# Linear attention and two dense layers on one core: scores in four array parts, one state run moved, states in other banks, weight loads later

## The chip, the cores and the metric

The kernel runs on one NeuronCore of a Trainium2 chip. Its engines work side by side, each through its own instructions in order: TensorE (PE in the profile; PEld is its weight load), VectorE (DVE), ScalarE (ACT), GpSimd (POOL), and SyncE (SP), which issues nearly all DMA transfers here. SBUF is the core's memory; PSUM has eight banks of 128 x 512 float32 that TensorE writes to. The metric is the device time of one execution in microseconds, lower is better.

## The reference

```python
for b in range(12):                       # blocks of 64 positions; 2 batches, 8 heads, 64 dims
    intra = einsum('bhic,bhjc->bhij', qb, kb) * Dmask      # Dmask = lam ** (i - j), i >= j
    intra = einsum('bhij,bhjd->bhid', intra, vb)
    inter = einsum('bhid,bhde->bhie', qb * lam_pow, kv_state)
    out[b] = intra + inter
    kv_state = lam_block * kv_state + einsum('bhsd,bhse->bhde', kb * rev_pow, vb)
x = out as 1536 x 512
g = elu(x @ w_in)                         # w_in 512 x 2048
x = g @ w_out                             # w_out 2048 x 512
x = softplus(x @ w_in2) @ w_out2          # the same shapes
```

## The kernel before

The attention is done in 12 chunks of 128 positions, six for each batch, with 8 heads as 4 pairs. For a chunk, `att_s` (line 296) makes the scores: 8 float32 matmuls of 64 rows and 128 columns, the even head of a pair from partitions 0 to 63 and the odd one from 64 to 127, into two PSUM banks of `ps_y`. `att_mask` multiplies them on VectorE with the decay mask (line 319). `att_x` (line 323) makes the output transposed in two banks of the ring `ps_h` of four: first the part from the state ("inter", line 334), in 64x64 parts of the array, which the first chunk of a batch does not have, then the part inside the chunk ("intra", line 343). `att_conv` splits the output into a high part on ScalarE (`xh`, line 357) and a rest on VectorE (`xl`, line 358). `att_state` (line 360) makes keys times values (line 370), VectorE adds the faded old state (line 376), GpSimd fades the new one; the last chunk of a batch makes no state. GpSimd scales the next q (`att_prep`), ScalarE (line 284) and GpSimd (line 291) scale the next k.

The order is written out by hand: `attention()` (line 539) issues for chunk g the scores and masking of chunk g+1, its scalings, then x, state and conversion of chunk g. The program order is the order on each engine. A float32 matmul shows as two records in the trace.

Behind the attention stand the two dense layers. Each of their matmuls is done in three products of a high part and a rest (lines 407 to 409 and 480). The weights come as packed words; for each, ScalarE converts twice (lines 111, 112), VectorE shifts and rounds up (lines 116, 122), ScalarE makes the high part (line 125) and VectorE the rest (line 128). Before the first steps of the MLP this is done in halves of a weight (`split_half`, five pieces), and `PIECES` says how many of the pieces of which half stand ahead of `att_x` and behind the conversion in each chunk. (0, 0) is the first half of weight 0, which `m1(0)` needs, (1, 0) that of weight 1. The halves of steps 0 to 4 of the MLP are split inside `early_step`. The first Relu (line 418) and what follows it on ScalarE stand behind the high part of (2, 0).

`LOADS` orders all loads on SyncE's queue: ("q", g) is q and k of a chunk transposed, ("k", g) is k and v, ("w", f, i) half i of weight f; each is 512 KB. The numbers ahead of the lists are the chunks behind which they are issued.

Of the kernel before, what the change touches and what calls it, by code (L numbers as in the profile page):

```python
# [7 lines left out]
F32 = mybir.dt.float32  # L8
# [7 lines left out]
P = 128  # L16
B, H, S, D = 2, 8, 768, 64
NPAIR = H // 2
CPB = S // P
NCHUNK = B * CPB  # L20
# [3 lines left out]
TT = 512  # L24
# [12 lines left out]

LOADS = {
# [4 lines left out]
}  # L43

STARTS = (
# [3 lines left out]
def body(ctx, tc, consts, attqk, attkv, w1, w2, out):  # L49
    nc = tc.nc  # L50
    V, A, G, T = nc.vector, nc.scalar, nc.gpsimd, nc.tensor
# [9 lines left out]
    ps_y = ctx.enter_context(tc.tile_pool(name="ps_y", bufs=1, space=PSUM))  # L61
# [16 lines left out]
    def bank(name):  # L78
        return ps_h.tile([P, TT], F32, tag="h", name=name)
# [89 lines left out]
    def split_half(fc, i):  # L169
        r, c = [x[:, :DM] for x in conv_tiles()]  # L170
        convert(whalf.pop((fc, i)), r, c)
        yield
        shift(r)
        yield
        round_up(r, c)
        yield
        if (fc, 0) not in wh:
            weight_tiles(fc)
        high(r, wh[fc, i])
        yield  # L180
        rest(c, wh[fc, i], wl[fc, i])
# [3 lines left out]
    def half(fc, i, count):  # L185
        if (fc, i) not in halves:
            halves[fc, i] = split_half(fc, i)
        for _ in range(count):
            next(halves[fc, i], None)
# [13 lines left out]
    def setup():  # L203
        A.dma_start(out=const_t, in_=consts)
        A.preload_act_table_set("natural_log_exp_and_others")
        warm(8)
        loads(0)

    def decays():
        for h in range(H):  # L210
            V.tensor_tensor_scan(  # L211
                out=dmask[:, h % 2, h // 2, :], data0=lam_t[:, h:h + 1].to_broadcast([P, P]), data1=id_t,
                initial=0.0, op0=ALU.mult, op1=ALU.add,
            )
        for e in range(2):
            A.activation(out=kdecay[:, e::2], in_=dmask[:, e, :, P - 1], func=AF.Copy)

    def powers():
        G.tensor_copy(qpow[:, :, :1], lam_t[:, H:].unsqueeze(2))
        for w in (1, 2, 4, 8, 16, 32, 64):  # L220
            G.tensor_tensor(
                out=qpow[:, :, w:2 * w], in0=qpow[:, :, :w],
                in1=qpow[:, :, w - 1:w].to_broadcast([P, NPAIR, w]), op=ALU.mult,
            )
# [6 lines left out]
    def loads(g):  # L231
        for load in LOADS.get(g, ()):
            {"q": att_load, "k": att_load_kv, "w": load_half}[load[0]](*load[1:])
# [27 lines left out]
    def att_prep(g):  # L261

        if g < NCHUNK and g % CPB:
            q = at[g][0].rearrange("p (a i) -> p a i", a=NPAIR)
            G.tensor_tensor(out=q, in0=q, in1=qpow, op=ALU.mult)


    def att_turn_k():
        ps = bank("kps")
        for p in range(NPAIR):  # L270
            o = slice(P * p, P * p + P)
            T.matmul(ps[:, o], at[0][1][:, o], id_t, start=True, stop=True, is_transpose=True, skip_group_check=True)  # L272
        return ps

    def k_heads(g):
        return H if g < 3 else H // 2

    def att_prep_k(g, source=None):
        if g >= NCHUNK or g % CPB == CPB - 1:
            return  # L280
        k = at[g][2].rearrange("p (h d) -> p h d", h=H)
        y = k if source is None else source.rearrange("p (h d) -> p h d", h=H)
        for h in range(k_heads(g)):
            A.activation(out=k[:, h], in_=y[:, h], func=AF.Copy, scale=kdecay[:, h:h + 1])

    def att_prep_k2(g):
        if g >= NCHUNK or g % CPB == CPB - 1 or k_heads(g) == H:
            return
        k = at[g][2].rearrange("p (h d) -> p h d", h=H)
        r = slice(k_heads(g), H)  # L290
        G.tensor_tensor(
            out=k[:, r], in0=k[:, r], in1=kdecay[:, r].unsqueeze(2).to_broadcast([P, H - k_heads(g), D]), op=ALU.mult)
# [3 lines left out]
    def att_s(g):  # L296

        if g >= NCHUNK:
            return
        q, k = at[g][:2]  # L300
        ps = [ps_y.tile([P, 512], F32, tag=f"y{g % 2 * 2 + e}", name=f"sps{e}") for e in range(2)]
        for p in range(NPAIR):
            o = slice(P * p, P * p + P)
            for e in range(2):
                r = slice(64 * e, 64 * e + 64)
                T.matmul(ps[e][:, o], k[r, o], q[r, o], start=True, stop=True, skip_group_check=True)  # L306
        sc[g] = ps

    def att_mask(g):
        if g >= NCHUNK:  # L310
            return
        ps = sc[g]
        sc[g] = s = ap2.tile([P, 2, NPAIR, P], F32, tag="sc", name="sc")
        part = 2 if g == 0 else NPAIR
        for a in range(0, NPAIR, part):
            r = slice(a, a + part)
            for e in range(2):
                y = ps[e].rearrange("p (a i) -> p a i", a=NPAIR)
                V.tensor_tensor(out=s[:, e, r], in0=y[:, r], in1=dmask[:, e, r], op=ALU.mult)
# [3 lines left out]
    def att_x(g):  # L323
        a = at[g]
        ps = [bank("xps") for e in range(2)]
        first = g % CPB == 0

        for p in range(0 if first else NPAIR):
            i = slice(P * p, P * p + P)
            o = slice(P * (p // 2), P * (p // 2) + P)  # L330
            for e in range(2):
                r = slice(64 * e, 64 * e + 64)
                c = 64 * (e ^ p & 1)
                T.matmul(  # L334
                    ps[e][c:c + 64, o], state[g - 1][r, p, :], a[0][r, i],
                    start=(p < 2), stop=False, skip_group_check=True,
                )
        for p in range(NPAIR):
            o = slice(P * (p // 2), P * (p // 2) + P)
            for c in range(2):  # L340
                e = c ^ p & 1
                h = 2 * p + e
                T.matmul(  # L343
                    ps[e][64 * c:64 * c + 64, o], a[3][:, D * h:D * h + D], sc[g][:, e, p, :],
                    start=first, stop=True, skip_group_check=True,
                )
        return ps
# [12 lines left out]
    def att_state(g):  # L360

        if g % CPB == CPB - 1:
            return
        a = at[g]
        ps = bank("stps")[:, :NPAIR * D]
        for p in range(NPAIR):
            for e in range(2):
                r = slice(D * e, D * e + D)
                o = slice(P * p + D * e, P * p + D * e + D)
                T.matmul(ps[r, D * p:D * p + D], a[2][:, o], a[3][:, o], start=True, stop=True, skip_group_check=True)  # L370
        ps = ps.rearrange("p (a i) -> p a i", a=NPAIR)
        state[g] = ap2.tile([P, NPAIR, D], F32, tag="state", name="state")
        if g % CPB == 0:
            V.tensor_copy(state[g], ps)
        else:
            V.tensor_tensor(out=state[g], in0=ps, in1=faded.pop(g - 1), op=ALU.add)  # L376
        if g % CPB < CPB - 2:
            faded[g] = ap2.tile([P, NPAIR, D], F32, tag="faded", name="faded")
            decay = qpow[:, :, P - 1:P].to_broadcast([P, NPAIR, D])
            G.tensor_tensor(out=faded[g], in0=state[g], in1=decay, op=ALU.mult)  # L380
# [153 lines left out]

    PIECES = {5: ((), (0, 0)), 6: ((0, 0), ()), 7: ((0, 0), ()), 8: ((0, 0), (1, 0)), 9: ((1, 0), ()), 10: ((1, 0), ()), 11: ((1, 0), ())}

    def attention():
        setup()  # L540
        powers()
        decays()
        att_s(0)
        att_prep_k(0, att_turn_k())
        att_mask(0)
        for g in range(NCHUNK):
            before, behind = PIECES.get(g, ((), ()))
            att_s(g + 1)
            att_mask(g + 1)
            att_prep(g + 1)  # L550
            att_prep_k2(g + 1)
            if before:
                half(*before, 1 if g in (6, 9) else 2)
            ps = att_x(g)
            att_state(g)
            att_conv(g, ps)
            att_prep_k(g + 1)
            if behind:
                half(*behind, 1)
            loads(g or None)  # L560
# [101 lines left out]
```

## Time and profile before

| | us |
|---|---|
| three runs | 571.41, 571.55, 571.59 (median 571.55) |
| the profiled execution | 571.56 |
| its span in the trace | 569.4 |
| TensorE busy | 563.9 (99%) |
| ScalarE / VectorE / GpSimd busy | 361.2 / 341.8 / 164.8 |
| attention, up to the first MLP matmul | 42.82 |

The time of an execution has 2.16 us around the span. [...] The DMA queue is full from 10 to 44 us (page part 2 and the windows: a share of 1.03 and 406 to 411 GB/s from 10 to 40 us). In the timeline a row is a group of like instructions: start, length to the end of the last, engine, line, operation, written tile <- read tiles, array part, shape, count; in brackets the idle time ahead of it and what ended that.

### The profile page before, as it was taken

To read this page: it belongs to the slowest core of one execution; us is meant where nothing else is said; L and a number is where in the kernel's file an instruction comes from. 1 tells how busy PE (TensorE), PEld (TensorE's weight loads), DVE (VectorE), ACT (ScalarE), POOL (GpSimd) and SP (SyncE) were. 2 spreads that over 40 slices of the span, in tenths; PEclk is the share of its full clock that TensorE was granted. 3 is DMA by queue.
4 is the path that set the end of the run, shared out by engine and by line. 5 is a ranking of instruction groups with operands and counts; after the bars stand their busy time and mean duration, and the time that the engine had idled before them with its cause. 6 is when DMAs were issued, how large, how long until landed. Compare 5 with 4: busy or idle time off the path is not lost.

```text
span 569.4 us, 7780 instructions
## 1 busy us (share of the span) xinstructions
PE 563.9 (99%) x3031; PEld 468.9 (82%) x3031; DVE 341.8 (60%) x407; ACT 361.2 (63%) x597; POOL 164.8 (29%) x143
## 2 busy tenths in 40 slices
PE   9999999999999999999999999999999999999997
PEld 8888888888888888888888888888888888888886
DVE  6797445545464444012767867665789855656656
ACT  5569657756566564333886976756899756655562
POOL 4661312222122122531532442122221221222210
PEclk9999999999999999999999999999999999999999
DMA  8992211423123222000332101100232000100202
GB/s 325 407 406 81 102 74 75 147 87 136 75 76 146 74 74 75 1 1 1 148 122 101 74 12 63 49 26 2 79 143 74 2 0 1 74 1 0 75 0 74
DMA packets 10692, 49.58 MB, mean 87 GB/s; under 512 B 1184, under 2 KB 1568, under 8 KB 7072
## 3 DMA queue, kind: packets, MB, share of 16 engines
q1 hardware_dynamic: 10368, 48.89, 22.7%
q8 instruction: 23, 0.38, 0.3%
q10 hardware_dynamic: 288, 0.20, 0.2%
q14 instruction: 13, 0.11, 0.1%
HBM read 45.95 MB, written 3.15 MB: 86 GB/s over the span
## 4 chain that ended last, share of the span: by engine, by line
PE 98%; DVE 1%; DMA 0%; issue 0%; DVEq 0%
PE y L480 45%; PE hps L407 15%; PE hps L409 15%; PE hps L408 15%; PE sps L306 2%; PE xps L343 2%; PE xps L334 1%; PE stps L370 1%; DMA const_t<-consts 0%; DVE dmask L211 0%; DVE yacc L527 0%; DVE yacc L482 0%; PE kps L272 0%; DVE state L376 0%; DVE yacc L519 0%
## 5 line engine op out<-in xcount | busy, mean ns | idle before, releaser
L407 PE MATMUL hps<-xh,wh 128*128 128x512 f32 x384 | 149.5, 389 | 0.0
L409 PE MATMUL hps<-xh,wl 128*128 128x512 f32 x384 | 149.5, 389 | 0.0
L408 PE MATMUL hps<-xl,wh 128*128 128x512 f32 x384 | 149.4, 389 | 0.0
L449 POOL TENSOR_TENSOR g<-v,g 128x512 fp32r<-128x512 f32 x48 | 62.9, 1311 | 193.4 <-ACT g L447 193.4
L480 PE MATMUL y<-g,wh 128*128 128x512 f32 x384 | 118.1, 389 | 0.0
L480 PE MATMUL y<-wh,g 128*128 128x512 f32 x382 | 117.7, 389 | 0.0
L449 POOL TENSOR_TENSOR g<-l,g 128x512 fp32r<-128x512 f32 x46 | 60.0, 1305 | 183.6 <-ACT g L447 164.2
L418 ACT ACTIVATE v<-hps 128x512 f32<-128x512 f32 x48 | 28.7, 597 | 98.8 <-PE hps L409 98.7
L442 DVE SCALAR_TENSOR_TENSOR v<-v,hps 128x512 f32<-128x512 f32 x48 | 33.0, 687 | 90.8 <-ACT v L419 90.7
L409 PEld LDWEIGHTS hps<-xh,wl 128*128 128x128 f32 x384 | 72.0, 188 | 15.1 <-DVE wl L128 0.2
L407 PEld LDWEIGHTS hps<-xh,wh 128*128 128x128 f32 x384 | 72.1, 188 | 15.1 <-issue 0.2
L408 PEld LDWEIGHTS hps<-xl,wh 128*128 128x128 f32 x384 | 72.1, 188 | 15.0
L480 PEld LDWEIGHTS y<-wh,g 128*128 128x128 f32 x382 | 71.7, 188 | 15.4 <-POOL g L449 0.2
L480 PEld LDWEIGHTS y<-g,wh 128*128 128x128 f32 x384 | 72.0, 188 | 14.9
L444 DVE TENSOR_TENSOR l<-l,u 128x512 f32<-128x512 f32 x48 | 75.2, 1566 | 4.7 <-DVE u L436 0.5
L436 DVE SCALAR_TENSOR_TENSOR u<-u,e 128x512 f32<-128x512 f32 x48 | 33.6, 700 | 69.4 <-ACT l L430 69.4
L480 PE MATMUL y<-g,wl 128*128 128x512 f32 x192 | 74.7, 389 | 0.0
L480 PE MATMUL y<-wl,g 128*128 128x512 f32 x191 | 74.3, 389 | 0.0
L427 ACT ACTIVATE e<-hps 128x512 f32<-128x512 f32 x48 | 28.6, 597 | 71.2 <-PE hps L409 71.2
L128 DVE TENSOR_TENSOR wl<-c,wh 128x1024 fp32r<-128x1024 f32 (+1 forms) x36 | 50.1, 1392 | 14.5 <-ACT wh L125 13.9
L122 DVE CUSTOM_DVE_ANT_0 c<-r,c 128x2048 uint16<-128x2048 uint16 (+1 forms) x36 | 40.7, 1130 | 4.7 <-ACT c L112 1.8
L480 PEld LDWEIGHTS y<-g,wl 128*128 128x128 f32 x192 | 36.1, 188 | 7.6
(70 smaller groups left out, 606.2 us busy)
## 6 DMA issues: line engine op xcount, KB each, us to landing
raw<-w SPq DMA_DIRECT2D x28, 1024.0 KB, 4.8
early<-attkv SPq DMA_DIRECT2D x8, 512.0 KB, 10.3
raw<-w SPq DMA_DIRECT2D x8, 512.0 KB, 10.2
qk<-attqk SPq DMA_DIRECT2D x6, 512.0 KB, 8.1
early<-attqk SPq DMA_DIRECT2D x6, 512.0 KB, 11.0
out<-yacc SPq DMA_DIRECT2D x7, 256.0 KB, 2.0
kv<-attkv SPq DMA_DIRECT2D x3, 512.0 KB, 10.1
out<-o SPq DMA_DIRECT2D x4, 256.0 KB, 2.3
```

The source lines that it names most:

```text
L122: V.tensor_tensor(out=c, in0=r.bitcast(U32), in1=c, op=ALU.add)
L128: V.tensor_tensor(out=lo, in0=c.bitcast(F32), in1=hi.bitcast(F32), op=ALU.subtract)
L407: T.matmul(ps, wh[fc, 0][:, o], h[:, k, :], start=(k == 0), stop=False)
L408: T.matmul(ps, wh[fc, 0][:, o], l[:, k, :], start=False, stop=False)
L409: T.matmul(ps, wl[fc, 0][:, o], h[:, k, :], start=False, stop=(k == KD - 1))
L418: A.activation(out=v, in_=ps, func=AF.Relu, scale=-1.0)
L427: A.activation(out=e, in_=ps, func=AF.Abs)
L436: V.scalar_tensor_tensor(out=u, in0=u, scalar=-1.0, in1=e, op0=ALU.add, op1=ALU.subtract)
L442: V.scalar_tensor_tensor(out=v, in0=v, scalar=-1.0, in1=ps, op0=ALU.add, op1=ALU.max)
L444: V.tensor_tensor(out=v, in0=v, in1=u[0], op=ALU.subtract)
L449: eng.tensor_tensor(out=g[:, 1], in0=v, in1=g[:, 0].bitcast(F32), op=ALU.subtract)
L480: T.matmul(yps[m], a, b, start=(c == begin and i == 0), stop=(last and i == 2))
```

## The change

Five things are changed. The scores are made in 16 matmuls of 64 rows and 64 columns, whose outputs lie in the four quarters of two banks. The scores of every chunk but chunk 1 go to banks y0 and y1 (chunk 1: y2 and y3), where even and odd chunks took turns. The state of every chunk but chunk 0 goes to y3 or y2 in place of a bank of the ring. For chunk 10 the state run and its addition stand directly behind the scores of chunk 11, ahead of their masking and of chunk 10's x. The first halves of weights 0 and 1 are loaded later in the queue, and their pieces are done later: those of (0, 0) in chunks 7 to 10 (before 5 to 8), those of (1, 0) in chunks 10 and 11 (before 8 to 11). The last four halves are issued behind chunk 10 in place of 9. GpSimd takes over three of eight heads of k's scaling in chunk 1 and four in chunk 2, which ScalarE did alone.

```diff
     0: (... ("q", 5), ("k", 4),
-        ("q", 6), ("k", 5), ("w", 0, 0), ("q", 7), ("k", 6), ("q", 8), ("k", 7), ("w", 1, 0)),
-    3: (("q", 9), ... ("k", 11), ("w", 2, 0), ("w", 0, 1)),
+        ("q", 6), ("k", 5), ("q", 7), ("k", 6), ("q", 8), ("k", 7), ("w", 0, 0)),
+    3: (("q", 9), ... ("k", 11), ("w", 1, 0), ("w", 2, 0), ("w", 0, 1)),
...
     def k_heads(g):
-        return H if g < 3 else H // 2
+        return {0: H, 1: 5}.get(g, H // 2)
...
-        ps = [ps_y.tile([P, 512], F32, tag=f"y{g % 2 * 2 + e}", name=f"sps{e}") for e in range(2)]
+        ps = [ps_y.tile([P, 512], F32, tag=f"y{2 * (g == 1) + e}", name=f"sps{e}") for e in range(2)]
         for p in range(NPAIR):
             o = slice(P * p, P * p + P)
-            for e in range(2):
+            for e, c in ((0, 0), (1, 1), (0, 1), (1, 0)):
                 r = slice(64 * e, 64 * e + 64)
-                T.matmul(ps[e][:, o], k[r, o], q[r, o], start=True, stop=True, skip_group_check=True)
+                i = slice(64 * c, 64 * c + 64)
+                T.matmul(ps[e][i, o], k[r, o][:, i], q[r, o], start=True, stop=True, skip_group_check=True)
...
-        ps = bank("stps")[:, :NPAIR * D]
+        if g:
+            ps = ps_y.tile([P, TT], F32, tag=f"y{2 + g % 2}", name="stps")[:, :NPAIR * D]
+        else:
+            ps = bank("stps")[:, :NPAIR * D]
...
-    PIECES = {5: ((), (0, 0)), 6: ((0, 0), ()), 7: ((0, 0), ()), 8: ((0, 0), (1, 0)), 9: ((1, 0), ()), 10: ((1, 0), ()), 11: ((1, 0), ())}
+    PIECES = {
+        7: ((), (0, 0)), 8: ((0, 0), ()), 9: ((0, 0), ()), 10: ((0, 0), (1, 0)), 11: ((1, 0), ())}
...
+            early = g == NCHUNK - 2
             att_s(g + 1)
+            if early:
+                att_state(g)
...
-                half(*before, 1 if g in (6, 9) else 2)
+                half(*before, {8: 1, 11: 4}.get(g, 2))
             ps = att_x(g)
-            att_state(g)
+            if not early:
+                att_state(g)
```

TensorE at the end of the attention, from the last scores (`sps`) of chunk 11 to the first MLP matmul (`hps`). Before:

```order
L306 MATMUL sps_743<-qk 128x128
L334 MATMUL xps<-qk,state 64x128 x8
L343 MATMUL xps<-sc,early 64x128 x8
L370 MATMUL stps<-early 64x64 x8
L334 MATMUL xps<-qk,state 64x128 x8
L343 MATMUL xps<-sc,early 64x128 x8
L407 MATMUL hps<-xh_227,wh_580 128x512
```

Now:

```order
L307 MATMUL sps_816<-qk 64x128
L374 MATMUL stps<-early 64x64 x8
L335 MATMUL xps<-qk,state 64x128 x8
L344 MATMUL xps<-sc,early 64x128 x8
L335 MATMUL xps<-qk,state 64x128 x8
L344 MATMUL xps<-sc,early 64x128 x8
L411 MATMUL hps<-xh_243,wh_773 128x512
```

The state run (`stps`) of chunk 10 moved from behind chunk 10's x to ahead of it.

TensorE at the scores of chunk 3, with the semaphores that an instruction waits on (DMAHW a load, DVE VectorE). Before:

```order
L306 MATMUL sps_298<-early 128x128 [waits DMAHW6_49]
L306 MATMUL sps_299<-early 128x128
L306 MATMUL sps_298<-early 128x128
L306 MATMUL sps_299<-early 128x128
L306 MATMUL sps_298<-early 128x128
```

Now:

```order
L307 MATMUL sps_316<-early 64x128 [waits DMAHW6_49,DVE_49]
L307 MATMUL sps_317<-early 64x128 [waits DVE_49]
L307 MATMUL sps_316<-early 64x128
L307 MATMUL sps_317<-early 64x128
L307 MATMUL sps_316<-early 64x128
```

The outputs have half as many partitions, and the first matmul into each bank waits for VectorE, which reads the chunk before out of the same bank.

ScalarE from chunk 9's conversion to the first Relu of the MLP (`xh2` is the output's high part, `early` the scaled k, `r`, `c` and `wh` the pieces of a weight half). Before:

```order
L357 ACTIVATE xh2_669<-xps_700 128x2x128
L284 ACTIVATE early_416<-early_416,kdecay_93 128x64 [waits DMAHW1_49]
L284 ACTIVATE early_416<-early_416,kdecay_93 128x64 x3
L125 ACTIVATE wh1_757<-r_679 128x512 [waits DVE_49]
L357 ACTIVATE xh2_669<-xps_760 128x2x128 [waits PE_49]
L357 ACTIVATE xh2_669<-xps_761 128x2x128
L357 ACTIVATE xh2_669<-xps_794 128x2x128 [waits PE_49]
L357 ACTIVATE xh2_669<-xps_795 128x2x128
L111 ACTIVATE r_838<-raw_420 128x512 [waits DMAHW3_49,Activation_49]
L112 ACTIVATE c_839<-raw_420 128x512
L125 ACTIVATE wh2_844<-r_838 128x512 [waits DVE_49]
L418 ACTIVATE v_848<-hps_825 128x512 [waits PE_49]
```

Now:

```order
L358 ACTIVATE xh2_739<-xps_849 128x2x128 [waits PE_49]
L358 ACTIVATE xh2_739<-xps_850 128x2x128
L111 ACTIVATE r_871<-raw0_141 128x512 [waits DMAHW2_49]
L112 ACTIVATE c_872<-raw0_141 128x512
L125 ACTIVATE wh1_881<-r_871 128x512 [waits DVE_49]
L358 ACTIVATE xh2_739<-xps_885 128x2x128 [waits PE_49]
L358 ACTIVATE xh2_739<-xps_886 128x2x128
L111 ACTIVATE r_929<-raw_455 128x512 [waits DMAHW3_49,Activation_49]
L112 ACTIVATE c_930<-raw_455 128x512
L125 ACTIVATE wh2_935<-r_929 128x512 [waits DVE_49]
L422 ACTIVATE v_939<-hps_916 128x512 [waits PE_49]
```

The two conversions of (1, 0) and its high part (`wh1`) moved in between the `xh` of chunk 10 and the `xh` of chunk 11.

## Rows read from the trace of the kernel before

**Rows 1.** The page, part 4: chain that ended last, shares of the span.
```profile
PE 98%; DVE 1%; DMA 0%; issue 0%; DVEq 0%
```
**Rows 2.** Timeline, TensorE, chunks 4 and 5: start, length, engine, line, operation.
```profile
16.06 1.16 PE L306 MATMUL sps<-early 64*128 64x128 f32 x16
17.15 0.67 PE L334 MATMUL xps<-early,state 64*64 64x128 f32 x16
17.75 1.09 PE L343 MATMUL xps<-sc,early 128*64 128x128 f32 x16
18.67 0.63 PE L370 MATMUL stps<-early 128*64 128x64 f32 x16
19.24 1.16 PE L306 MATMUL sps<-early 64*128 64x128 f32 x16
...
24.10 1.09 PE L343 MATMUL xps<-sc,early 128*64 128x128 f32 x16
25.13 0.38 PE L306 MATMUL sps<-early 64*128 64x128 f32 x2
```
**Rows 3.** Timeline, TensorE, from chunk 11's scores to the first MLP matmul.
```profile
37.26 1.16 PE L306 MATMUL sps<-qk 64*128 64x128 f32 x16
...
39.87 0.63 PE L370 MATMUL stps<-early 128*64 128x64 f32 x16
41.20 0.67 PE L334 MATMUL xps<-qk,state 64*64 64x128 f32 x16 [0.69 <-DVE state L376]
...
42.82 0.50 PE L407 MATMUL hps<-xh,wh 128*128 128x512 f32 x1
```
**Rows 4.** Groups by form, weight loads, 0 to 45 us: busy us, mean ns.
```profile
L334 PEld LDWEIGHTS xps<-qk,state 64*64 64x64 f32 x80 | 2.2, 132 | 1.3 <-issue 0.8
```
**Rows 5.** Timeline, VectorE, one chunk in steady state.
```profile
16.27 0.42 DVE L376 TENSOR_TENSOR state<-stps,faded 128x256 f32<-128x256 f32 x1 [0.89 <-PE stps L370]
16.61 0.75 DVE L358 TENSOR_TENSOR xl<-xps,xh 128x256 fp32r<-128x256 f32 x2
17.28 1.28 DVE L319 TENSOR_TENSOR sc<-sps,dmask 128x512 f32<-128x512 f32 x2
```
**Rows 6.** Timeline, SyncE: issues of two loads, one behind the other.
```profile
23.99 0.33 SPq L258 DMA_DIRECT2D kv<-attkv  x1
25.27 0.33 SPq L250 DMA_DIRECT2D qk<-attqk  x1
```
**Rows 7.** Timeline, ScalarE, from chunk 8's scaling to the first Relu of the MLP.
```profile
31.66 1.06 ACT L284 ACTIVATE kv<-kv,kdecay 128x64 f32<-128x64 f32 x4 [0.47 <-DMA kv<-attkv]
...
37.45 1.05 ACT L284 ACTIVATE early<-early,kdecay 128x64 f32<-128x64 f32 x4
...
42.93 0.66 ACT L357 ACTIVATE xh<-xps 128x256 fp32r<-128x256 f32 x2 [2.19 <-PE xps L343]
43.48 0.68 ACT L111 ACTIVATE r<-raw 128x512 f32<-128x512 f32 x1
...
44.65 0.63 ACT L125 ACTIVATE wh<-r 128x512 fp32r<-128x512 f32 x1
45.89 0.60 ACT L418 ACTIVATE v<-hps 128x512 f32<-128x512 f32 x1 [0.61 <-PE hps L409]
```
**Rows 8.** Timeline, VectorE, the pieces of weight halves in the first MLP steps.
```profile
44.19 0.43 DVE L116 TENSOR_SCALAR r<-r 128x512 uint32<-128x512 uint32 x1
44.76 0.69 DVE L122 CUSTOM_DVE_ANT_0 c<-r,c 128x1024 uint16<-128x1024 uint16 x1
45.55 0.69 DVE L128 TENSOR_TENSOR wl<-c,wh 128x512 fp32r<-128x512 f32 x1
...
52.67 1.56 DVE L128 TENSOR_TENSOR wl<-c,wh 128x512 fp32r<-128x512 f32 x1 [0.16 <-ACT wh L125]
```
**Rows 9.** Timeline, TensorE, second and third matmul of early step 3.
```profile
54.08 0.39 PE L408 MATMUL hps<-xl,wh 128*128 128x512 f32 x1
54.30 0.47 PE L409 MATMUL hps<-xh,wl 128*128 128x512 f32 x1
```

4 rows, old and new, of the table LOADS are left out of this document.

## The prediction

> **What bounds the kernel now.** The chain of work that ended last is matmul time for 98% of the span [rows 1]: TensorE is the bound, and the change is worth what it takes out of TensorE's own sequence, plus or minus the few places where TensorE waits. So I read the timeline of TensorE next. One chunk of the attention in steady state is four runs of 16 records (8 matmuls, each in two records): scores (L306), the part from the state (L334, "inter"), the part inside the chunk (L343, "intra"), the new state (L370). They start at 16.06, 17.15, 17.75, 18.67, and the next chunk's scores at 19.24 [rows 2]: 1.09 + 0.60 + 0.92 + 0.57 = 3.18 us, with no wait. At the end stands the one wait of weight: the inter run of chunk 11 waits 0.69 us for the state of chunk 10 [rows 3]. After it TensorE runs the MLP with hardly a gap, so a microsecond gained before the first MLP matmul at 42.82 is a microsecond of the kernel, unless an early MLP step loses it again.
>
> **What a run costs.** Intra to state keeps the same division of the array (128*64 in both), and intra takes 0.92. Where another division follows (chunk 5 has no state), intra takes 25.13 - 24.10 = 1.03 [rows 2]. So a change of division costs about 0.11 at its end. Inter works in four 64*64 parts and holds 16 records in 4 rounds; less 0.11 it takes 0.49. Intra holds 16 records in two parts, 8 rounds, in 0.92. The difference of 4 rounds is 0.43, so a round is 0.108 and a start after a change of division costs 0.06. The state run's 8 short rounds are then 0.57 - 0.11 = 0.46.
>
> **Scores in four parts.** The matmuls double to 16 a chunk (32 records), but four run at a time: again 8 rounds. They stand in the same division and the same pattern of banks as the inter run behind them, so nothing is paid between the two. Scores become 8 x 0.108 + 0.06 = 0.92; inter becomes 4 x 0.108 + 0.11 = 0.54, without its start. Together 1.46 where 1.69 stood: 0.23 less. No row shows a 64*64 score run; the inter run is nearest (same parts, same 128 columns) and I take it. Scores are followed by inter eight times before the end (chunks 2 to 6 and 8 to 10): 8 x 0.23 = 1.84. The scores of chunks 1 and 7 are followed by intra and keep the 0.11: 0.92 + 0.11 against 1.09, 0.06 each, 0.12. Those of chunk 0 I leave at nothing, with 0.1 as the bound.
>
> **State of chunk 10 ahead of its x.** From the scores of chunk 11 to the first MLP matmul: 42.82 - 37.26 = 5.56 now [rows 3]. Then it is scores 0.92 + 0.11, state 0.06 + 0.46 + 0.11, and twice inter (0.06 + 0.43 + 0.11) and intra (0.92 + 0.11): 1.03 + 0.63 + 2 x 0.60 + 2 x 1.03 = 4.92. The wait of 0.69 is gone, since the state's addition has inter and intra of chunk 10 to hide behind (1.63); a little is paid back because the state run stands alone between two changes of division. What is late next is the scaled k: the state run starts 1.03 after the scores instead of 39.87 - 37.26 = 2.61. ScalarE scales the first four heads from 37.45 to 38.50 [rows 7], 1.24 after the scores' start, and that hangs on chunk 9's x and does not come sooner. Matmuls on the first head can go, those on the fourth cannot: 0 to 0.3 lost, I take 0.1. So 0.64 - 0.10 = 0.54. On VectorE the mask of chunk 11 now queues behind this state's addition; it should end some 3.5 after the scores' start, and its intra run comes at 1.03 + 0.63 + 0.60 + 1.03 + 0.60 = 3.89.
>
> **Banks.** State runs leave the ring of four for y2 and y3; that removes waits which cost nothing. In exchange, from chunk 3 on the scores always use y0 and y1, and wait until VectorE has masked the chunk before. That mask ends at 17.28 + 1.28 = 18.56, 2.50 after its scores' start [rows 5]; the next scores come at 3.18 now and at 2.95 then. Spare: 0.45. Queued behind the wait is all of TensorE. A weight piece of 0.43 or 0.69 [rows 8] falls into the idle 0.89 ahead of the state's addition [rows 5], which shrinks to 0.66, so chunk 9 may be 0.1 late. Cost taken: nothing, bound 0.3.
>
> **Loads.** One load takes a slot of 1.28 us on a full queue (issues at 23.99 and 25.27, [rows 6]). The first half of weight 0 and then of weight 1 go behind attention loads, so q of chunk 7 and all attention loads after it land one slot sooner. That is not a gain now; it is a cover. ScalarE's scaling for chunk 8 waits already for its load at 31.66 [rows 7], and TensorE will be 5 x 0.23 + 0.12 + 0.23 = 1.5 ahead there: without the slot the state run behind that scaling could come to wait. With it 1.28 of the 1.5 is covered; the 0.2 left over is the bound, and I take nothing.
>
> **Weight pieces, and where some of the gain goes.** Weight 1's first half is now split by ScalarE and VectorE in chunks 10 and 11 instead of 8 to 11. Call the first MLP matmul M. Chunk 10's intra starts 1.03 + 0.60 + 1.03 = 2.66 ahead of M and lasts 1.09, so ScalarE takes its xh at M - 1.54. Then, with the distances of [rows 7]: the two conversions at M - 0.99 and M - 0.44; VectorE, busy until then with weight 0's rest and chunk 10's xl, shifts at M - 0.20; the high part goes at M + 0.25; only then comes xh of chunk 11, at M + 0.80 where it is at M + 0.11 now. VectorE follows with round-up at M + 0.34, rest at M + 1.12 (0.79 behind it, as 44.76 to 45.55 in [rows 8]), two xl, and weight 2's shift at M + 2.40 to 2.83. Weight 2's high part starts at M + 2.86 (now M + 1.83) and the first Relu of the MLP at M + 3.39, where it is at M + 3.07 now, after 0.61 of idle time that is thus used up. So ScalarE falls 0.32 behind. From that Relu on it has no gap until the high part of weight 3, and TensorE waits already a little for weight 3's rest (52.67 + 1.56 = 54.23 in [rows 8]; the third matmul at 54.30 takes 0.47 where its neighbour takes 0.39, [rows 9]). The 0.32 therefore comes back in full as a wait there. Bounds: 0, and 0.69 if the whole delay of xh passes on.
>
> **Sum.** 1.84 + 0.12 + 0.54 = 2.50 at M, which comes at about 40.3; less 0.32 is 2.18. The profiled execution took 571.56 (its span 569.4 and 2.16 around it), the median of the three runs 571.55: 571.56 - 2.18 = 569.4.
>
> **Rivals.**
> *Rounds paced by weight loads.* A 64*64 load takes 132 ns [rows 4], more than a round of 108. If a round of scores lasted as long as its load, a run is 8 x 0.132 + 0.06 = 1.12: 0.03 saved in eight chunks (0.24), 0.14 lost in chunks 1 and 7 each (0.28), 0.20 lost at the end (0.34 of the 0.54 left). 0.30 in all, and ScalarE's 0.32 takes it: 571.5. Against it: inter has the same loads and holds its four rounds in 0.43. [...]
> *Masking becomes the bound.* If the mask ended 0.45 late in every chunk, the scores would wait in each and the chunk return to 3.18; the 1.84 goes and 0.34 is left: 571.2. For it: one pair of banks instead of two. Against it: 0.89 of idle VectorE per chunk. [...]
> *Two parts on the same rows do not overlap.* The two column halves of one head stream the same q columns from the same partitions; in the inter run the parts that share partitions stream different columns, so no row shows this case. If they took turns, scores are 16 rounds: 16 x 0.108 + 0.06 = 1.79. Then 8 x (1.79 + 0.54 - 1.69) = 5.1 lost, 2 x 0.81 in chunks 1 and 7, 0.9 in chunk 0, 0.3 at the end: 7.9, so 579.5, slower. It decides from a round of 0.108 + (2.18 + 1.1) / 96 = 0.142 on (12 chunks of 8 rounds). Against it: nothing in inter's rows distinguishes the streams.
>
> **How the numbers follow.** The forecast has 0.82, the loads 0.07, the mask 0.05, the streams 0.06. The forecast's own range: with no lag of ScalarE, no wait for k and 0.1 from chunk 0 it is 569.4 - 0.32 - 0.1 - 0.1 = 568.9; with a lag of 0.69 for 0.32, 0.3 for 0.1 at k, 0.3 for the banks and 0.2 for the loads, 570.5. That holds nearly all of the 0.82; since the upper ends will hardly all come together, I give 568.8 to 570.4. About 0.2% (1.1 us) is what a measurement of this kernel tells from no change. Faster by more: 0.83; within: 0.11 (most of loads and mask); slower: 0.06.
>
> **What would show it.** In the changed profile: scores to inter 0.92, inter to intra 0.54, chunk to chunk 2.95; scores with no wait for the masking; no wait of inter for the state; first MLP matmul near 40.3; the first Relu 3.4 after it; a wait of some 0.4 at the third matmul of early step 3, for weight 3's rest. Scores at 1.1 would point to the loads, at 1.8 to the streams, a wait for the mask in each chunk to the banks. A first MLP matmul at 40.3 with a total above 570.4 would mean that the early MLP steps gave back more than I worked out.

## The result, and the profile after

The changed kernel takes **579.99 us** (median of five runs, 579.31 to 580.52) where the kernel before takes 571.55 in the same comparison: a ratio of 1.0148, with a 95% interval of 1.0133 to 1.0162. It is slower by 8.4 us; the forecast was 569.4, range 568.8 to 570.4. The profiled execution took 580.52, its span 578.7.

The page of after, parts 2 to 4, answers to [rows 1]: the granted clock in 40 slices, the queue that carries instructions (packets, MB, share of 16 engines), and the chain that ended last.
```profile
PEclk9998999999999999999999999999999999999999
...
q8 instruction: 25, 0.41, 0.3%
...
PE 94%; issue 2%; ACT 2%; DVE 1%; DMA 0%; DVEq 0%; ACTq 0%
```
"issue" is time in which TensorE waited for nothing that the profile shows. It is 2% of the chain where it was 0%; rounded as it is, that stands for some 9 to 14 us, a loss of the right size. What TensorE (and its weight loads) waited for, summed by line, longest in the last column:
```profile
PE xps L335 <- issue: 5.0, 3, 2.2
PE stps L374 <- issue: 1.8, 1, 1.8
PE sps L307 <- issue: 1.3, 2, 0.9
```
Three different lines wait, 8.1 us in six pauses, and none of the six names another engine. The timeline of TensorE, one undisturbed chunk and the first pauses behind it (as [rows 2]):
```profile
16.14 1.10 PE L307 MATMUL sps<-early 64*64 64x128 f32 x32
17.07 0.62 PE L335 MATMUL xps<-early,state 64*64 64x128 f32 x16
17.62 1.09 PE L344 MATMUL xps<-sc,early 128*64 128x128 f32 x16
18.54 0.40 PE L374 MATMUL stps<-early 128*64 128x64 f32 x7
20.71 0.46 PE L374 MATMUL stps<-early 128*64 128x64 f32 x9 [1.78 <-issue]
```
Scores to inter is 0.93 and inter to intra 0.55, as forecast (0.92 and 0.54). Then the state run stops after 7 of its 16 records. The stop is not at a seam of the program: the same run of matmuls goes on 1.78 later. The end of the attention, as [rows 3]:
```profile
39.97 0.99 PE L307 MATMUL sps<-qk 64*64 64x128 f32 x27 [0.88 <-issue]
...
42.92 1.10 PE L307 MATMUL sps<-qk 64*64 64x128 f32 x32
43.95 0.83 PE L374 MATMUL stps<-early 128*64 128x64 f32 x16
44.72 0.32 PE L335 MATMUL xps<-qk,state 64*64 64x128 f32 x1
47.20 1.13 PE L335 MATMUL xps<-qk,state 64*64 64x128 f32 x15 [2.16 <-issue]
48.26 1.97 PE L344 MATMUL xps<-sc,early 128*64 128x128 f32 x16
50.16 0.73 PE L335 MATMUL xps<-qk,state 64*64 64x128 f32 x16
50.82 1.09 PE L344 MATMUL xps<-sc,early 128*64 128x128 f32 x16
51.85 0.50 PE L411 MATMUL hps<-xh,wh 128*128 128x512 f32 x1
```
M, the first MLP matmul, stands at 51.85, where it was 42.82 and was forecast at 40.3. The pauses stand ahead of TensorE's matmul records number 221, 347, 473, 600, 726 and 853 (counted from 0): every 126 or 127 records, whatever the line. And there is a second loss behind the last of them. By stretches (length, busy us of each engine with its records, then granted clock, DMA share, GB/s):
```profile
45.00:47.20 2.20, 0.04 (x2) 0.01 (x2) 2.12 (x4) 0.00 (x0) 0.46 (x1) 0.94 0.16 61
47.20:48.26 1.06, 1.06 (x16) 0.73 (x16) 0.00 (x0) 0.00 (x0) 0.00 (x0) 0.50 0.00 0
48.26:50.16 1.90, 1.90 (x20) 1.57 (x17) 0.00 (x0) 0.00 (x0) 0.00 (x0) 0.50 0.03 9
50.16:51.85 1.69, 1.69 (x35) 1.35 (x33) 1.07 (x3) 1.57 (x4) 0.00 (x0) 0.94 0.00 0
```
After standing idle for 2.16 us TensorE ran at a granted clock of 0.50, where the mean over the span of the kernel before is 1.000. Inter took 1.06 for 0.60, intra 1.90 for 1.03, the next inter 0.66 for 0.60: 1.4 us. From the forecast M to this one it is 11.55: these 1.4, and 10.15 left over, which is what the runs with a pause in them are longer than their undisturbed like (10.2 by their rows; the 8.1 of idle time leave out what the modelled end of the matmul ahead covers).

**What stands every 126 records.** A matmul record goes with a weight load (3223 of each, page part 1), so 126 of them are some 252 instructions. The trace has each DMA packet: on q8 there is one of 16,384 bytes for each such block. Those of the attention start at 11.34, 18.27, 24.57, 31.22, 37.19 and 45.02, take 0.9 to 1.1 us, and the pauses end at 13.84, 20.71, 27.05, 33.63, 39.97 and 47.20: 1.2 to 1.8 behind the end of a packet, four times 1.3 to 1.4. In the trace of before the same packets end 1.9 to 3.4 ahead of their first use. So the theory, FETCH: TensorE's instructions come in blocks through the DMA engines that also carry the loads; from the end of one pause to the end of the next it is 6.3 to 7.2 us here; the chunks of before used a block up in 126 / 64 x 3.18 = 6.3, the changed ones in 126 / 80 x 2.96 = 4.7. The packets start 3.6 to 5.1 behind the start of the block before, so while it is used up; by FETCH, one that is used up before the next has come ends in a pause.

### The profile page after: what moved, and what is told of

Read it like the earlier page. It is cut to its first block, busy times and chain, and to the rows that moved or that the text cites. A ratio compares the mean times of both kernels' runs of the same rounds, so it can differ in the third digit from the quotient of the medians.

```text
span 578.7 us, 8163 instructions
## 1 busy us (share of the span) xinstructions
PE 565.8 (98%) x3223; PEld 469.5 (81%) x3223; DVE 341.4 (59%) x407; ACT 359.5 (62%) x590; POOL 166.1 (29%) x145
## 4 chain that ended last, share of the span: by engine, by line
PE 94%; issue 2%; ACT 2%; DVE 1%; DMA 0%; DVEq 0%; ACTq 0%
PE y L484 44%; PE hps L413 15%; PE hps L412 15%; PE hps L411 15%; PE sps L307 2%; PE xps L344 2%; PE xps L335 1%; PE stps L374 1%; DMA const_t<-consts 0%; DVE wl L128 0%; ACT wh L125 0%; ACT r L111 0%; ACT c L112 0%; DVE yacc L531 0%; DVE dmask L211 0%
## 5 line engine op out<-in xcount | busy, mean ns | idle before, releaser
L431 ACT ACTIVATE e<-hps 128x512 f32<-128x512 f32 x48 | 28.6, 597 | 71.0 <-PE hps L413 71.0
## 6 DMA issues: line engine op xcount, KB each, us to landing
early<-attqk SPq DMA_DIRECT2D x6, 512.0 KB, 10.8
kv<-attkv SPq DMA_DIRECT2D x3, 512.0 KB, 10.1
```

The lines of the kernel that those rows point to most:

```text
L431: A.activation(out=e, in_=ps, func=AF.Abs)
```

## Experiments

Rivals at the start: **ISSUE RATE** (so many instructions cannot be issued faster, loads or not) and **BANKS** (something in the move of the states to y2 and y3, not in the scores). A third, that the streams do not overlap, has fallen already: it wanted scores of 1.79, and they take 0.92.

**One part undone: the scores in two parts again.**
```diff
-            for e, c in ((0, 0), (1, 1), (0, 1), (1, 0)):
+            for e in range(2):
...
-                T.matmul(ps[e][i, o], k[r, o][:, i], q[r, o], start=True, stop=True, skip_group_check=True)
+                T.matmul(ps[e][:, o], k[r, o], q[r, o], start=True, stop=True, skip_group_check=True)
```


> The changed kernel with the scores back in two 64x128 parts (8 matmuls a chunk); banks, moved state, loads and pieces stay as changed. Theory FETCH: TensorE's instructions come in blocks of 126 matmul records over the DMA engines, and with the data queue full a block lands some 6 to 7 us after the block before it begins; four-part scores use a block up in about 4.7 us. With 64 records a chunk again a block lasts 6.2 us and the gaps go: 571.4 us (0.5 gained at the end of the attention, 0.3 lost to ScalarE's lag), at most one short gap. Rival BANKS (scores on one pair of banks wait for the masking, which stays changed here): still 577 to 580. Rival ISSUE RATE (TensorE cannot issue that many small instructions whatever the DMA does): also 571.4.

Measured: 571.53, ratio 1.0001 [0.9992, 1.0011]. One pause of 0.41 is left, M is 42.40. BANKS falls: with all else changed, the loss is gone without the four-part scores. FETCH and ISSUE RATE forecast the same here.

**That part alone on the kernel before** (the same lines the other way).

> The kernel before with nothing changed but the scores in four 64x64 parts (16 matmuls a chunk). FETCH and ISSUE RATE: the gaps of the changed kernel appear, one every 126 matmul records between 13 and 47 us, and the time is 578 to 581 us. BANKS: the pairs of banks still take turns, so no gaps, and about 569.8 us (0.23 in each of eight chunks).

Measured: 576.57, ratio 1.0090 [1.0075, 1.0105], with five pauses for "issue" of 0.6 to 1.4. BANKS falls here too. The direction is that of FETCH, the size is not: 5.1 us, where 578 to 581 was expected. The rest waits for the run with the loads undone, below.

**The DMA engines emptied.** From chunk 3 on, the tiles of the chunk three before are used again (and k and v of chunk 2 lie in another buffer).
```diff
     def att_load(g):
+        if g > 2:
+            at[g] = at[g - 3][:2]
+            return
...
     def att_load_kv(g):
+        if g > 2:
+            at[g] += at[g - 3][2:]
+            return
```


> The changed kernel without the loads of q, k and v from chunk 3 on: these chunks work on the tiles of three chunks before, so their data is wrong, while every instruction of the compute engines stays. The DMA queue is then nearly empty from about 15 us on. FETCH: a block comes in time, the gaps go, and the time is what the prediction's sum gives, 569.4 us (568.8 to 570.2). ISSUE RATE: the gaps stay, 578 to 580. BANKS: 578 to 580.

> The kernel before without the loads of q, k and v from chunk 3 on, as the control of the run with few loads: these chunks work on older tiles. FETCH: the kernel before has no gap, its blocks last 6.3 us and come just in time, so nothing changes: 571.5 us, within 0.3. ISSUE RATE and BANKS: the same.

Measured: 569.27, ratio 0.9962 [0.9949, 0.9975], for the changed kernel; 571.31, ratio 1.0001 [0.9991, 1.0010], for the kernel before. What TensorE waited for in the changed kernel without the loads:
```profile
PE sps L313 <- DMA qk<-attqk: 0.6, 1, 0.6
PE sps L313 <- issue: 0.4, 1, 0.4
```
The end of its attention, in the timeline:
```profile
38.84 0.67 PE L341 MATMUL xps<-qk,state 64*64 64x128 f32 x16
39.43 1.09 PE L350 MATMUL xps<-sc,early 128*64 128x128 f32 x16
40.46 0.50 PE L417 MATMUL hps<-xh,wh 128*128 128x512 f32 x1
```
The same instructions at the same rate run without a pause once the engines are free: ISSUE RATE falls. The one pause left, 0.39 at 13.28, lies where the first loads still run. From 18 to 33 us, where no load stands in the way, the packet of a block starts 0.2 to 0.8 behind the start of the block before it, and 2.1 behind it at both ends, where loads run; in the changed kernel with its loads it is 3.6 to 5.1. The kernel before does not change without the loads, so it is not their absence alone that wins time.

M is 40.46, near the 40.3 of the forecast, but two things cancel in it. Chunk 0's scores took 1.03 in this profiled execution and 1.77 in that of before, so chunk 1's scores start 0.69 sooner (6.44 for 7.12); and the one pause lengthens its run of scores and inter from 1.48 to 2.17. From chunk 1's scores to M it is 34.02 where it was 35.69: 1.67 less, 2.36 without the pause, for the 2.50 of the sum. The sum comes out within 0.14 for a kernel that gets its instructions.

**Is it the length of the data queue, or that the engines are busy?** Some eight loads of 512 KB are under way: from 10 to 36 us they land 10.1 to 10.8 behind their issue (medians by line), at a slot of 1.28 each [rows 6]. A wait on SyncE holds each back until the load three (or five) before has landed; the same bytes are moved. The wait is also put on the two-part kernel and on the kernel before. The edit, shortened (the loads of k and v and of the weights get the same):
```diff
+    issued = []
+    def paced(load):
+        if len(issued) >= 3:
+            tc.add_manual_dep(load.ins, issued[-3], ...)
+        issued.append(load.ins.name)
...
-        nc.sync.dma_start(out=qk, in_=attqk[g])
+        paced(nc.sync.dma_start(out=qk, in_=attqk[g]))
```


> The changed kernel, with one thing added: each load of q, k, v and of a half of weights waits on SyncE until the load three before it has landed, so that at most three loads of 512 KB stand in the data queue where some eight did. The same bytes are moved, so a share of the DMA engines is all that an instruction block can get, but it finds a short queue ahead of it. DEPTH (a block of TensorE's instructions comes late because of the many transfers already queued on the 16 engines): its packet starts within 1.5 us of the block before, as without the loads, the pauses shrink to under 0.5 us each and the time is 569.4 to 571.5. SHARE (it comes late because the engines are busy at all, however many loads are queued): packets start 3 to 6 us behind as now, pauses of 1 to 2 us stay, and the time is 578 to 581. If three loads do not keep the engines busy, attention waits for its data, and the time is longer with pauses that name loads.

> The same with five loads instead of three. DEPTH: the block's packet starts later than with three and sooner than with eight; pauses of some 0.5 to 1 us, 572 to 577. SHARE: 578 to 581, as with three and with eight.

> The changed kernel with the scores put back into two parts (64x128, 8 matmuls) and at most three loads in the queue. It took 571.5 with eight, with one pause of 0.41. DEPTH: the pause goes, 571.0 to 571.3. SHARE: 571.5. Either way it gives the cost or gain of the short queue where instructions are not short.

> The kernel before with at most three loads in the queue; a control. Its blocks came just in time, so there is no pause to win. DEPTH and SHARE: 571.5 within 0.5; the packets of instructions start sooner by DEPTH (under 1.5 us behind the block before, where it is 2.4 to 3.6), unmoved by SHARE. Above 572.5 the short queue itself costs, by loads that come late, and the two runs on the changed kernel have to be read with that.

Measured: 578.65 (three), 577.91 (five), 579.16 (two parts, three), 579.30 (before, three); ratios 1.0125, 1.0100, 1.0133 and 1.0139, each within 0.003. With three loads on the changed kernel, the queue of the loads from 10 to 36 us (packets, MB, share of 16 engines):
```profile
q1 hardware_dynamic: 2215, 8.05, 90.6%
```
Its longest wait, in the timeline of TensorE:
```profile
36.12 1.20 PE L316 MATMUL sps<-qk 64*64 64x128 f32 x28 [3.00 <-DMA qk<-attqk]
```
And with five loads, the largest line of what TensorE waited for:
```profile
PE xps L344 <- issue: 6.1, 3, 3.3
```
With three no pause for instructions is left, but the loads run at 310 GB/s where it was 406, and TensorE waits for q, k and v instead; these waits also stretch four of the five blocks to 5.4 us and more, which gives their packets time. With five the loads keep 406 GB/s, and the pauses stay: 7.9 us of idle time in the profiled execution, which was the slowest of its four (576.10 to 580.31). The loss is 6.5 us for 8.4.

Both controls missed their forecast of 571.0 to 572.0 by over 7 us: the short queue costs by itself. The kernel before loses 8 us with it, 6.5 us of that in waits that name q, k and v or the scaling of q, the rest mostly in a lower clock behind them (0.50 at 30.40 to 32.00, behind a wait of 2.32). So with three loads the four-part kernel (578.65) is level with the two kernels of two parts (579.16, 579.30): what the four parts cost is gone, and the price of the short queue stands in its place.

That is neither DEPTH nor SHARE as I wrote them. From eight loads to five the packets start no sooner; from five to three the length of the queue and the rate of the loads fall together, and no run tells the two apart. That the engines have some idle time is not enough: the last block's packet started 5.1 behind the start of the block before in the changed kernel, at a DMA share of 0.90 (39.97 to 45.02), and 6.0 behind it with five loads, at 0.82 (38.77 to 44.77).

**The 3.4 us between 576.6 and 580.0.** Only the order and place of the weight loads and pieces are put back; of that edit the loads are shown.
```diff
-        ("q", 6), ("k", 5), ("q", 7), ("k", 6), ("q", 8), ("k", 7), ("w", 0, 0)),
-    3: (..., ("k", 11), ("w", 1, 0), ("w", 2, 0), ("w", 0, 1)),
-    10: (("w", 3, 0), ("w", 1, 1), ("w", 2, 1), ("w", 3, 1)),
+        ("q", 6), ("k", 5), ("w", 0, 0), ("q", 7), ("k", 6), ("q", 8), ("k", 7), ("w", 1, 0)),
+    3: (..., ("k", 11), ("w", 2, 0), ("w", 0, 1)),
+    9: (("w", 3, 0), ("w", 1, 1), ("w", 2, 1), ("w", 3, 1)),
...
```


> The changed kernel with one part undone: order and place of the weight loads, and with them the pieces of weight, are those of before; four-part scores, early state and banks stay. It asks where the last 3.3 us come from (579.9 against 576.6 of the kernel before with four-part scores alone): a pause of 2.16 ahead of chunk 10's inter run and the half clock of TensorE behind it. LATE LOADS (weight halves issued at 38 to 39 keep the engines busy at 40 to 46, when the last block of the attention is fetched): the pause shrinks to under 1, the clock stays at 1.00, and the time is 575.5 to 577. NOT THE LOADS (the last block comes late in any case with the early state): pause and half clock stay, 579 to 580.5.

Measured: 576.19, ratio 1.0080 [1.0066, 1.0093]. The end of its attention, in the timeline of TensorE:
```profile
43.57 0.83 PE L374 MATMUL stps<-early 128*64 128x64 f32 x16
44.34 0.95 PE L335 MATMUL xps<-qk,state 64*64 64x128 f32 x16
45.22 0.99 PE L344 MATMUL xps<-sc,early 128*64 128x128 f32 x14
```
Three stretches of it, with the columns of the stretches above:
```profile
41.00:43.00 2.00, 2.00 (x53) 1.88 (x52) 1.64 (x4) 0.81 (x4) 1.84 (x2) 1.00 0.97 356
43.00:45.00 2.00, 2.00 (x53) 1.60 (x48) 1.30 (x5) 1.31 (x5) 1.77 (x2) 1.00 0.49 191
45.00:47.00 2.00, 2.00 (x45) 1.48 (x39) 1.95 (x4) 0.64 (x2) 0.08 (x1) 1.00 0.03 8
```
And two of the changed kernel:
```profile
39.00:42.00 3.00, 2.12 (x57) 1.86 (x57) 1.84 (x5) 1.51 (x6) 1.46 (x3) 1.00 0.89 236
42.00:45.00 3.00, 3.00 (x75) 2.54 (x71) 2.20 (x6) 1.60 (x6) 2.87 (x4) 1.00 0.83 277
```
The forecast of LATE LOADS holds: the packet of the last block starts at 42.01, not 45.02, the pause is down to an inter run of 0.88 for 0.60, and the half clock is gone. So the changed order of the loads, costed at nothing, cost 3.8 us of the 8.4 in this company. The reason that LATE LOADS gives does not hold: that packet started while the engines were still full (0.97), and the one of the changed kernel came 5.1 behind the start of the block before, 2.6 later than here, at the lower share of 0.83 to 0.89. In the changed kernel three weight halves had been issued just before, at 38.1 to 39.0, and its packet started only behind the landing of the first of them, at 44.33. Why it waited so long is not shown.

**Half the dose, and the state alone.** Four parts in even chunks only; and the kernel before with nothing but the early state.
```diff
-            for e, c in ((0, 0), (1, 1), (0, 1), (1, 0)):
-                i = slice(64 * c, 64 * c + 64)
+            for e, c in ((0, 0), (1, 1), (0, 1), (1, 0)) if g % 2 == 0 else ((0, None), (1, None)):
+                i = slice(64 * c, 64 * c + 64) if c is not None else slice(0, P)
```
```diff
             att_s(g + 1)
+            early = g == NCHUNK - 2
+            if early:
+                att_state(g)
...
-            att_state(g)
+            if not early:
+                att_state(g)
```


> The changed kernel with four-part scores in the chunks of even number alone, two parts (8 matmuls) in the others. A chunk has 72 records on average in some 3.07 us, so a block of 126 lasts 5.4 us where it lasts 4.7 with four parts everywhere and 6.2 with two. FETCH (blocks come every 6 us or so while the data queue is full): pauses still stand every 126 records, shorter by some 0.7 each; 573 to 576.5. If each four-part run brought its own pause, pauses would stand at even chunks alone and not at 126 records, with a time of 575 to 576.

> The kernel before with nothing but the state of chunk 10 computed ahead of its x; state runs stay in the ring of four banks, scores have two parts, loads are those of before. The prediction's sum gives this part 0.54 at the first matmul of the MLP; TensorE has as many instructions as before. If that holds: first MLP matmul 42.2 to 42.4 and 570.9 to 571.3. FETCH: the same, since no instruction is added; a block that comes up to 0.5 late would take the gain back, 571.5.

Measured: 572.67, ratio 1.0020 [1.0010, 1.0029], for even chunks; a little less than expected. Its longest pause, in a chunk whose scores have two parts:
```profile
30.96 1.16 PE L307 MATMUL sps<-qk 64*128 64x128 f32 x16
32.05 0.43 PE L335 MATMUL xps<-early,state 64*64 64x128 f32 x3
33.30 0.66 PE L335 MATMUL xps<-early,state 64*64 64x128 f32 x13 [0.81 <-issue]
```
So a pause belongs to the block, not to the run: records 599 and 725 pause, each 126 apart again. Counted by how much longer the runs take, four pauses cost 2.95 there (two of them are hidden from the idle time by the modelled ends).

The state alone: 571.32, ratio 0.9999 [0.9990, 1.0007], that is, not told from no change. In its profile:
```profile
37.37 1.16 PE L306 MATMUL sps<-qk 64*128 64x128 f32 x16
38.46 0.78 PE L370 MATMUL stps<-early 128*64 128x64 f32 x16
39.17 0.67 PE L334 MATMUL xps<-qk,state 64*64 64x128 f32 x16
...
42.41 0.50 PE L407 MATMUL hps<-xh,wh 128*128 128x512 f32 x1
```
M is 42.41: from the scores of chunk 11 it is 5.04 where it was 5.56 [rows 3]. The 0.54 of the sum is there (0.52), but chunk 11's scores begin 0.11 later, and 0.41 of 571 is under what the runs can tell.

**Between three and five, and both cures together.** At most four loads on the changed kernel; then four with even chunks and the loads as before; and four on the kernel with the early state alone.

> The changed kernel with at most four loads in the queue, between three (no pause for instructions, loads at 300 GB/s, 578.6) and five (full rate, pauses as with eight, 577.9). If the pauses go as soon as the engines idle a little, and the loads keep 350 GB/s or more: 572 to 576. If the pauses shrink only as far as the data slow down: 577 to 579, as on either side.

> The changed kernel with four-part scores in even chunks alone, weight loads and pieces as before, and at most four loads in the queue. SUPPLY (a block every 5.8 us on average against 5.4 in use): the pauses, 2.95 in all with a full queue, shrink to under 1; the first MLP matmul comes at 41.5 to 42.4, and the time is 570.2 to 571.2, under both kernels. LATE DATA (four loads in the queue bring q, k and v late for the attention, or weights late): waits that name loads, 572 to 575.

> The kernel before with the state of chunk 10 ahead of its x, as run alone, and at most four loads in the queue. It uses a block in 6.2 us, so by SUPPLY no pause is there to win and none comes: 571.0 to 571.5. LATE DATA: over 572, with waits that name loads.

Measured: 573.75, ratio 1.0028 [1.0011, 1.0045]; 572.62, ratio 1.0018 [1.0007, 1.0029]; 572.99, ratio 1.0032 [1.0017, 1.0047]. With four loads on the changed kernel the loads keep 359 GB/s and four pauses are left, 0.3 to 1.4, 3.3 us of idle time for 8.1: the first of the two cases. What TensorE waited for in the second of them (the second is put down to VectorE, but the q of chunk 7 landed at 24.71 and the scores started at 24.85):
```profile
PE sps L316 <- DMA qk<-attqk: 1.5, 1, 1.5
PE sps L316 <- DVE xl L368: 1.0, 1, 1.0
```
and in the third:
```profile
PE sps L315 <- DMA qk<-attqk: 1.6, 3, 0.8
PE xps L352 <- DMA early<-attkv: 1.2, 1, 1.2
```
By SUPPLY the pauses should shrink to under 1 in the second and none come in the third, and no row of either names "issue". But 2 to 3 us came back as waits for data. I had expected SUPPLY to hold alone, 570.2 to 571.2 and M at 41.5 to 42.4, and got 572.62 and 44.05; LATE DATA holds beside it. No version that makes all its loads is told faster than the kernel before.

The runs side by side. GB/s is that of the loads from 10 to 36 us; "packet" is how far behind the start of a block of 126 records the packet for the next one starts, in the attention from record 221 on (where a pause shows it, a block starts at the pause's end):

| kernel | GB/s | a block lasts unpaused, us | packet, us | M | median, us |
|---|---|---|---|---|---|
| before | 405 | 6.3 | 2.4 to 3.6 | 42.82 | 571.55 |
| changed | 406 | 4.7 | 3.6 to 5.1 | 51.85 | 579.99 |
| changed, loads as before | 406 | 4.7 | 2.4 to 4.2 | 47.86 | 576.19 |
| changed, even chunks | 406 | 5.4 | 3.0 to 4.1 | 44.31 | 572.67 |
| changed, queue of five | 406 | 4.7 | 3.4 to 6.0 | 51.87 | 577.91 |
| changed, queue of four | 359 | 4.7 | 2.6 to 4.4 | 45.61 | 573.75 |
| changed, queue of three | 310 | 4.7 | 1.6 to 2.5 | 49.39 | 578.65 |
| changed, few loads | 112 | 4.7 | 0.2 to 0.8, 2.1 beside loads | 40.46 | 569.27 |

M holds chunk 0's scores, whose length differs between profiled executions: chunk 1's scores start at 6.4 to 7.4 us.

The pauses of the changed kernel are worked out from it: 3.6 to 5.1 until the packet starts, 0.9 to 1.1 for the packet, 1.2 to 1.8 until its first instruction runs, together 6.3 to 7.2 against 4.7, so 1.6 to 2.5 for each block. Why its packets start later than those of before at the same rate of loads isn't shown.

## Why the prediction was wrong

**The step that failed** is in "Scores in four parts": "The matmuls double to 16 a chunk (32 records), but four run at a time: again 8 rounds." The rounds are right, and the 16 added records were costed by the time of the array alone. No term of the sum asks where the instructions come from. The trace of before could have been asked: by the packets of q8 a block was fetched within 2.4 to 3.6 + 1.05 + 1.35 = 4.8 to 6.0 us of the start of the one before, and was used up in 6.3. With 4.7 in its place, each block would have come 0.1 to 1.3 late. What the runs showed is more, 1.6 to 2.5 for each of the five blocks between the six pauses and 10.15 for all six, because the packets themselves started later (3.6 to 5.1). It was a resource nearly used up that no row of waits names, because nothing waited yet.

**Loads** failed as well. "That is not a gain now; it is a cover" counts the place of a load only for the data that it brings. With the weight halves moved to the end, the packet of the last block came 2.6 later behind the start of the block before: 579.99 - 576.19 = 3.8 for the moved loads and pieces together, of which 1.4 is the half clock behind a pause of 2.16.

**Right, by the runs that leave supply out.** Run lengths (0.93, 0.55), and 2.36 for 2.50 from chunk 1's scores to M with few loads. That the time comes so near, 569.27 for 569.4, is in part chance, as with M above. So the early state (0.52 for 0.54) and the four-part scores are sized right. No scores wait for a mask, and inter no longer waits for the state. What is late next is, as forecast, the scaled k: the state run of chunk 10, behind the scores of chunk 11, takes 0.77 for 0.63 (0.14, taken as 0.1). ScalarE's lag is there too: the first Relu of after starts 3.32 behind M (forecast 3.39, before 3.07 in [rows 7]), the chain that ended last runs over ScalarE and VectorE from 50.3 to 63.5 (ScalarE's 2% of it), and the third matmul of early step 3 waits, as the last of these rows shows against [rows 9]:
```profile
55.17 0.58 ACT L422 ACTIVATE v<-hps 128x512 f32<-128x512 f32 x1
```
```profile
62.86 0.39 PE L411 MATMUL hps<-xh,wh 128*128 128x512 f32 x1
63.09 0.39 PE L412 MATMUL hps<-xl,wh 128*128 128x512 f32 x1
63.53 0.50 PE L413 MATMUL hps<-xh,wl 128*128 128x512 f32 x1
```
From M to the last matmul it is 523.08 in the changed kernel and 522.82 before, 0.26 given back for the 0.32 of the sum. Every kernel here with the changed pieces has 523.1 or 523.2 (one 522.9), every one with the old pieces 522.7 to 522.8.

**The rivals.** Weight loads and masking did not happen. The rival of the streams gave 579.5, and the time is 580.0, but that is chance: it wanted scores of 1.79. The prediction's own tests would have told it: "A first MLP matmul at 40.3 with a total above 570.4", or scores at 1.1 or 1.8, are all absent; what came instead, M at 51.85 with every run at its forecast length, was on no list.

## What to carry to other kernels

When a change doubles the instructions of an engine to save array time, count instructions per microsecond against what the fetch brought before: the packets of the instruction queue, when they start, and how far ahead of their first use they end. Here that margin, 1.9 to 3.4 us in the kernel before, was spent where the loads filled the DMA engines (406 GB/s from 10 to 36 us), so judge a transfer's place also by the instruction blocks that it stands beside. A pause called "issue" at a fixed distance in instructions (126 or 127 matmul records), on whatever line, was the sign of it here.

## What the runs showed of the hardware

- By the packets of q8, TensorE had about one block of its instructions ahead: in the attention the packet for the next block started 0.2 to 6.0 us behind the start of the block before, and its first instruction ran 1.2 to 1.8 behind the packet's end where TensorE was waiting for it. In the MLP, where a block lasts 28.6 us, the packet ended 16 to 32 us ahead of the block's first instruction (kernel before and changed kernel).
- Blocks of 4.7 us were late at 406 GB/s of loads (8.1 us of idle time) and at 359 (3.3); at 310 no pause was left, though waits for data stretched most blocks there. Holding the loads to three in the queue gave back 1.3 of the changed kernel's 8.4 us and cost the kernel before 8: 310 GB/s, and waits for data.
- TensorE's clock was 0.50 behind idle times of 2.16 (changed kernel), 2.32 (before, queue of three), 3.00 (queue of three), 3.26 (queue of five) and 4.33 (two parts, queue of three); it was 1.00 behind those of 1.78 and 1.68 in the changed kernel and 1.55 in the run with even chunks and four loads. A pause of 2.16 thus cost 3.6.
